# Causal attention feeding a mixture of experts on one core: the wide score products of most pairs as three float32r products with a split on GpSimd, separate loads, and a new order of steps

## The chip, the cores and the metric

The kernel runs on 1 core of one Trainium2 chip. The metric is the device time of a run in microseconds (us). In the profile PE is TensorE's matmul, PEld its weight load, DVE is VectorE, ACT ScalarE, POOL GpSimd, SP SyncE.

## The reference

Inputs are q, k and v of 4 batches x 12 heads x 448 positions x 64, and the weights of 8 experts. Attention first, causal and in float32:

```python
scores = scale * np.matmul(q, k.transpose(0, 1, 3, 2))
scores = np.where(mask, -1000000000.0, scores)
scores = scores - np.max(scores, axis=-1, keepdims=True)
attn = np.exp(scores)
attn = attn / (np.sum(attn, axis=-1, keepdims=True) + 1e-09)
return np.matmul(attn, v).astype(np.float32)
```

Its output, as 1792 tokens of 768 numbers, goes to a layer of experts: each token takes the one expert with the highest cosine similarity to an embedding, and the layer gives `gate * (relu(x @ w1[e]) @ w2[e])`, with w1 of 768 x 1024 and w2 of 1024 x 768.

## The kernel before

The 48 heads are worked as 24 pairs. A pair is one tile `raws[p % 4]` of 128 partitions x 2 x 448: q and k, transposed, the first head in partitions 0 to 63 and the second in 64 to 127. The 448 queries are cut into four chunks of 112; because of the causal mask, chunk i needs 112 x (i + 1) keys, so its scores are 112, 224, 336 or 448 columns wide. Each pair p passes through these steps, whose names carry the pair behind a point:

- LD loads q and k into `raws` and v into `vts`, both rings of four, by two transfers on SP's queue; SP waits in order, the transfer of v for the PV products of four pairs before.
- S0 to S3 are the scores of a chunk (S02 takes chunks 0 and 2 in one step), on PE in float32: for each head one product over 64 partitions, the two heads in the two halves of the array.
- M, on DVE, adds the mask, scales and takes the row maximum (in0 from PSUM, in1 the mask in SBUF); E, on ACT, is the exp with its sum. M21 is chunk 2, head 1.
- T transposes on PE; V (x and y halves) copies the transposes from PSUM to SBUF on ACT or DVE, as the order says (/A or /V).
- PV0 to PV3 are the products with v; VO copies the result. RC adds a constant to the sums on GpSimd (/G) or DVE (/V) and takes the reciprocal on DVE. X is a product that turns the result and adds router logits; XE and LE scale it by the reciprocals, on DVE.

After each batch of six pairs, WX writes x to DRAM on SP's queue, the R steps choose experts (Rc, on DVE, compares two operands in SBUF), and the q steps sum squares on GpSimd. After the third batch the commonest expert ("star") is known: LW and LL load its weights, W and Wl split w1 into a rounded float32r part and a float32r rest (W on ACT, Wl on GpSimd but for the last), A and B the same for w2 on ACT and DVE. The F and G steps are the first expert products; each float32 product there is already made of three float32r products. Behind them loops over up to 20 more tiles of tokens follow.

The order of all this on every engine is the string ORDER, written out by an offline search: a token is a step, its pair, a PSUM bank and an engine. An engine runs its own part of the list in that order and waits by semaphores. `h1` and `l1` are the tiles that later hold the split of w1. The 16 transposes of an identity ahead of ORDER only warm PE.

Of the kernel before, what the change touches and what calls it, by code (L numbers as in the profile page):

```python
# [45 lines left out]
V3x.1/A E20.2 S3.3:2 M00.3 M01.3 M20.3 M21.3 T0.2:1 E31.2 es6.0 V0x.2/A PV0.1:7 M31.3 es7.0 es8.0 VO.0/A E21.2 PV1.1
PV2.1 PV3.1 E30.2 RC.0/G M30.3 es9.0:2 esA.0 V0y.2/A E01.3 E00.3 T2.2:0 S02.4:2 V2x.2/A V2y.2/V X.0:1 M01.4 M00.4
E11.3 M20.4 M21.4 T3.2:0 E10.3 V3x.2/A V3y.2/A LD.5 XE0.0 XE1.0 LE1.0 E31.3 S3.4:2 LE0.0 E20.3 M30.4 S1.4:1 T0.3:0
PV0.2:6 E30.3 PV1.2 M31.4 V0x.3/V V0y.3/V RC.1/G M10.4 PV2.2 M11.4 E21.3 PV3.2 VO.1/V T2.3:0 LD.6 E01.4 E10.4 V2x.3/V
T3.3:1 V2y.3/A S1.5:2 V3x.3/V X.1:0 V3y.3/A E00.4 E30.4 M10.5 VO.2/A E31.4 S02.5:1 M11.5 S3.5:2 E11.4 LE0.1 PV0.3:7  # L50
M01.5 PV1.3 M00.5 E21.4 RC.2/G PV2.3 M21.5 XE0.1 M31.5 E21.5 XE1.1 M20.5 E20.4 LE1.1 PV3.3 E11.5 T0.4:0 M30.5 V0x.4/A
T2.4:1 T3.4:2 V0y.4/V V2y.4/A V2x.4/V X.2:0 V3y.4/V LD.7 S02.6:1 V3x.4/A E10.5 E00.5 RC.3/G XE1.2 RC.4/G S3.6:2 E20.5
LE0.2 M01.6 M20.6 LE1.2 E31.5 M00.6 E30.5 PV0.4:6 VO.3/A M30.6 XE0.2 PV1.4 PV2.4 PV3.4 M21.6 T2.5:1 M31.6 E01.5 T0.5:2
V2x.5/V E00.6 V0y.5/V S1.6:0 M11.6 V2y.5/A T3.5:1 M10.6 V0x.5/A V3x.5/V S3.7:2 S02.7:0 E20.6 V3y.5/A LD.8 M30.7 X.3:1
M31.7 LE1.3 E30.6 M20.7 E31.6 S1.7:2 LE0.3 E01.6 M00.7 PV0.5:7 E10.6 E21.6 VO.4/A XE1.3 M21.7 PV1.5 M01.7 PV2.5 E11.6
XE0.3 RC.5/G M11.7 PV3.5 T0.6:0 M10.7 V0y.6/V E21.7 T2.6:1 V2x.6/V E01.7 S1.8:2 V0x.6/A V2y.6/A M10.8 M11.8 X.4:0
LE1.4 T3.6:1 S02.8:2 E20.7 E31.7 VO.5/A XE0.4 XE1.4 LE0.4 M01.8 V3y.6/A M00.8 LD.9 X.5:0 M21.8 V3x.6/A M20.8 E21.8
XE1.5 T2.7:1 S3.8:2 RC.6/G E10.7 V2y.7/V E00.7 E11.7 E01.8 M30.8 PV0.6:7 PV1.6 V2x.7/V E30.7 PV2.6 XE0.5 PV3.6 LE1.5
LE0.5 T3.7:1 E20.8 M31.8 RC.7/G V3y.7/V LD.10 T0.7:0 VO.6/A S3.9:2 V0y.7/V V3x.7/A S1.9:1 R0.5:7 V0x.7/A M31.9 S02.9:0
M01.9 E31.8 M11.9 M30.9 M20.9 M10.9 E00.8 E30.8 PV0.7:6 E11.8 M21.9 PV1.7 E10.8 X.6:2 T2.8:1 M00.9 E30.9 T0.8:0  # L60
# [1096 lines left out]
```

## Time and profile before

| | |
|---|---|
| median of 3 runs | 479.69 us (478.72 to 480.52) |
| profiled execution | 477.16 us, span 475.4 us |
| granted TensorE clock, mean | 0.994 |
| PE busy | 458.1 us (96%) |
| DVE busy | 347.5 us (73%) |
| ACT busy | 296.0 us (62%) |
| GpSimd (POOL) busy | 111.6 us (23%) |

Times inside the profile are counted from the start of the span. A matmul's busy time includes its way through the array and overlaps with the next one's, so how fast products follow each other is read from starts, and a busy PE is not a PE at its peak. A wait is put down to what released the engine last.

### The profile page before, as it was taken

Reading aid. Unit: us, or ns where it says so; the run is one execution under the profiler, and the core shown is the slowest. Engines: PE = TensorE matmul, PEld = TensorE weight load, DVE = VectorE, ACT = ScalarE, POOL = GpSimd, SP = SyncE. Lnnn points to the kernel's source line nnn. Section 1 sums busy time; section 2 is a strip of 40 time slices with the busy share of each in tenths; the row PEclk is TensorE's granted clock in tenths of the full one; section 3 lists DMA queues with packets and bytes.
Section 4 is the critical chain, followed back from the end, with each engine's and each line's share of the span. In section 5 each row is a group of like instructions: output and inputs, shape, how many; then the busy total and the mean of one; then the engine's idle time right before and its main releaser. Section 6 shows DMA issues by size and latency. Waiting matters only on the chain. (4 is left out here: it accounts for less than half of the span.)

```text
span 475.4 us, 12096 instructions
## 1 busy us (share of the span) xinstructions
PE 458.1 (96%) x3868; PEld 375.7 (79%) x3868; DVE 347.5 (73%) x1023; ACT 296.0 (62%) x729; POOL 111.6 (23%) x121
## 2 busy tenths in 40 slices
PE   7999999998999989999999999999999999999993
PEld 5666666675776778888998899989989988988972
DVE  4989988897899799535778786919988456677441
ACT  6999998897999875311368662729476531171531
POOL 3000244056076633210031210202021020010121
PEclk9999999999999999999999999999999999999997
DMA  7333361363467753111779628287877411837881
GB/s 237 96 119 118 126 225 61 118 198 99 133 217 254 264 185 101 34 68 45 289 267 392 218 99 299 70 307 294 309 268 264 137 42 38 325 135 269 306 283 38
DMA packets 27376, 87.32 MB, mean 184 GB/s; under 512 B 2694, under 2 KB 3142, under 8 KB 27280
## 3 DMA queue, kind: packets, MB, share of 16 engines
q1 hardware_dynamic: 24160, 72.38, 43.8%
q0 software_dynamic: 3120, 13.77, 8.1%
q8 instruction: 47, 0.77, 0.7%
q14 instruction: 49, 0.40, 0.3%
HBM read 144.33 MB, written 12.58 MB: 330 GB/s over the span
## 5 line engine op out<-in xcount | busy, mean ns | idle before, releaser
L400 ACT ACTIVATE aq<-aq,mx 112x336 f32<-112x336 f32 (+3 forms) x192 | 99.9, 528 | 5.0 <-DVE mx L395 4.9
L395 DVE CUSTOM_DVE_ANT_0 aq<-bank,ar 112x336 f32<-112x336 f32 (+3 forms) x192 | 76.5, 442 | 14.5 <-PE bank L390 13.9
L851 POOL DMA_INDIRECT out_dram<-fa,isx x18 | 24.9, 1386 | 180.7 <-DVEq L1042 46.8
L390 PE MATMUL bank<-ak 64*112 64x112 f32 (+3 forms) x384 | 58.0, 414 | 2.3 <-DMA ak<-in_qk_dram 1.5
L433 PE MATMUL bank<-ap 112*64 112x112 f32 (+3 forms) x384 | 52.3, 408 | 0.0
L797 ACT COPY fa<-bank 128x512 f32<-128x512 f32 x28 | 15.2, 588 | 57.2 <-PE bank L738 40.2
L696 DVE STREAM_TRANSPOSE turned<-fa 32x256 f32<-32x256 f32 x112 | 48.8, 435 | 1.5
L433 PEld LDWEIGHTS bank<-ap 112*64 112x64 f32 x384 | 24.5, 136 | 25.0 <-issue 15.5
L1005 DVE TENSOR_TENSOR wl<-fa,wh 128x1024 fp32r<-128x1024 f32 x36 | 41.5, 1220 | 3.1 <-PE bank L739 1.6
L422 ACT COPY ap<-bank 112x384 f32<-112x384 f32 (+2 forms) x87 | 38.6, 481 | 7.0 <-PE bank L418 5.5
L418 PEld LDWEIGHTS bank<-idt,aq 64*112 64x112 f32 (+1 forms) x960 | 33.5, 131 | 11.8 <-issue 2.7
L418 PE MATMUL bank<-idt,aq 48*112 48x48 f32 (+1 forms) x960 | 38.5, 219 | 0.9 <-DVE mx L395 0.7
L601 POOL DMA_INDIRECT fa<-xd,ig x21 | 23.2, 1103 | 64.5 <-PE bank L669 52.5
L400 ACT ACTIVATION_READ_ACCUMULATOR aq<-aq,mx 112x1 f32 x192 | 37.8, 197 | 0.0
L390 PEld LDWEIGHTS bank<-ak 64*112 64x112 f32 x384 | 28.3, 175 | 12.0 <-DVE mx L395 4.8
L1004 ACT CAST wh<-fa 128x1024 fp32r<-128x1024 f32 x36 | 34.9, 1047 | 3.5 <-PE bank L740 1.6
L740 PE MATMUL bank<-wh,akr 128*128 128x512 f32 x84 | 33.0, 393 | 0.8 <-DVE akr L650 0.8
L422 DVE COPY ap<-bank 112x384 f32<-112x384 f32 (+2 forms) x57 | 28.7, 521 | 6.6 <-PE bank L418 6.2
L738 PE MATMUL bank<-wh,akr 128*128 128x512 f32 x84 | 33.0, 393 | 0.0
L740 PE MATMUL bank<-wh,apr 128*128 128x512 f32 x84 | 32.9, 391 | 0.0
L739 PE MATMUL bank<-wl,akr 128*128 128x512 f32 x84 | 32.8, 391 | 0.0
L739 PE MATMUL bank<-wl,aor 128*128 128x512 f32 x84 | 32.8, 390 | 0.0
(312 smaller groups left out, 1076.0 us busy)
## 6 DMA issues: line engine op xcount, KB each, us to landing
fa<-in_w_dram SPq DMA_DIRECT2D x76, 768.0 KB
fa<-in_w_dram SPq DMA_DIRECT2D x54, 1024.0 KB
ak<-in_qk_dram SPq DMA_DIRECT2D x24, 448.0 KB
ap<-in_vv_dram SPq DMA_DIRECT2D x24, 224.0 KB
xd<-fa SPq DMA_DIRECT2D x3, 1344.0 KB
fa<-in_w_dram SPq DMA_DIRECT2D x6, 512.0 KB
xd<-fa SPq DMA_DIRECT2D x1, 1120.0 KB
fa<-xd,ig POOLq DMA_INDIRECT x21, 6.6
```

Source lines behind the costliest of these rows:

```text
L390: pe.matmul(o, raws[p % 4][rows, 0, CP * i : CP * i + CP], raws[p % 4][rows, 1, :n], start=True, stop=True, tile_position=(D * h, 0), skip ...
L395: v.tensor_tensor_reduce(out=Ps[p % 2][i, h], in0=st.pop(("sp", p, i, h)), in1=mask[i], scale=-0.125, scalar=3e38, op0=ALU.add, op1=ALU.mi ...
L400: ac.activation(x, x, AF.Exp, bias=mxs[p % 3][:, h, i : i + 1], scale=-1.0, accum_out=sums[p % 3][:, h, i : i + 1])
L418: pe.transpose(t[:, h, k], Ps[p % 2][i, h][r, c * CP : c * CP + CP], idt[r, r], tile_position=(r.start, 0))
L422: copy()(PTs[p % 2][:, :, slice(*GROUPS[n]), ROWS[half]], st["pt", p, n][half])
L433: pe.matmul(st["o", p][64 * h : 64 * h + 64, CP * c : S], vts[p % 4][:, c, 64 * h : 64 * h + 64], PTs[p % 2][:, h, RUNS[c]], start=c == 0, ...
L696: v.transpose(xk[32 * j : 32 * j + 32, :, q : q + 32], blocks[q : q + 32, :, j])
L738: pe.matmul(acc[j], xh[:, k], wh[k][:, o], start=k == ends[0], stop=False)
L739: pe.matmul(acc[j], xh[:, k], wl[k][:, o], start=False, stop=False)
L740: pe.matmul(acc[j], xl[:, k], wh[k][:, o], start=False, stop=k == ends[1])
L1004: ac.copy(h[k], r[:, k])
L1005: v.tensor_tensor(l[k], r[:, k], h[k], op=ALU.subtract)
```

## The change

It does four things. For pairs 1 to 20, the scores of chunks 2 and 3 (336 and 448 columns wide) are no longer one float32 product per head, but three float32r products summed in PSUM: high x high, high x low, low x high. The high and low parts are made by two new GpSimd steps, `hi` (a copy that rounds to float32r) and `lo` (the difference), over 672 columns: the queries from 224 on and all keys. They live in the first three tiles of `h1` and `l1`, used in turn. The load of q and k (LDr) is a step apart from that of v (LDv), and pair 0's is cut in two, with the first 224 columns (LDa) in front. And ORDER is new throughout; some of its lines are shown.

```diff
 ORDER = """
-EE.0 LD.0 S1.0:0 es0.0 M11.0 E11.0 LD.1 M10.0 E10.0 S02.0:1 M00.0 M01.0 M20.0 E00.0 M21.0 S3.0:2 M31.0 E01.0 S1.1:0
...
-M11.16 M10.16 T2.14:0 VO.13/V V2x.14/A X.12:1 S02.16:2 XE1.12 WX.11 V2y.14/A LE0.12 LE1.12 XE0.12 R1.11 M21.16 LD.17
...
+LDa.0 LDr.0 S1.0:1 EE.0 es0.0 S3.0:0 S02.0:2 M11.0 M10.0 M31.0 LDr.1 M30.0 M20.0 M21.0 S1.1:1 M01.0 hi.1 E10.0 E31.0
...
+V3y.1/V es4.0 M10.3 hi.3 V3x.1/A lo.3 S3.3:2 M11.3 es5.0 E31.2 S02.3:0 es6.0 M30.3 E01.2 hi.4 E20.2 T3.2:1 es7.0 M01.3
...
+LDv.15 E20.15 q0.11 E11.15 LDr.17 PV3.13 T0.14:1 V0y.14/V R0.11:6 LDr.19 T3.14:0 VO.13/A V0x.14/A V3y.14/A V3x.14/A
+X.12:2 XE0.12 S02.16:1 hi.17 E10.15 LE1.12 XE1.12 E01.15 E30.15 LE0.12 M20.16 M01.16 X.13:0 M21.16 hi.18 WX.11 E31.15
...
+M10.16 R2.11 RC.14/G lo.17 XE1.13 RC.15/G S1.17:2 XE0.13 qa0.11 V0y.15/A E20.16 M10.17 M11.17 T3.15:1 S3.17:0 V3y.15/A
...
-        @step("LD")
-        def _(p):
-            sy.dma_start(raws[p % 4], qk[p])
-            sy.dma_start(vts[p % 4], vv[p])
+        HALF = slice(0, 2 * CP), slice(2 * CP, S)
+        step("LDa", FIRST)(lambda p: sy.dma_start(raws[0][:, :, HALF[0]], qk[0][:, :, HALF[0]]))
+
+        @step("LDr")
+        def _(p):
+            c = slice(0, S) if p else HALF[1]
+            sy.dma_start(raws[p % 4][:, :, c], qk[p][:, :, c])
+
+        step("LDv")(lambda p: sy.dma_start(vts[p % 4], vv[p]))
+
+
+        SPLIT = range(1, NP - 3)
+        his, los = ([x[:, : 2 * CP + S] for x in xs_[:3]] for xs_ in (h1, l1))
+
+        def late(p):
+            return raws[p % 4].rearrange("p a s -> p (a s)")[:, 2 * CP :]
+
+        step("hi", SPLIT)(lambda p: g.tensor_copy(his[p % 3], late(p)))
+        step("lo", SPLIT)(lambda p: g.tensor_tensor(los[p % 3], late(p), his[p % 3], op=ALU.subtract))
 
         def scores(p, chunks):
...
                 n = CP * (i + 1)
-                for h in range(2):
-                    rows = slice(D * h, D * h + D)
-                    st["sp", p, i, h] = o = sp[h][:CP, at : at + n]
-                    pe.matmul(o, raws[p % 4][rows, 0, CP * i : CP * i + CP], raws[p % 4][rows, 1, :n],
-                              start=True, stop=True, tile_position=(D * h, 0), skip_group_check=len(chunks) > 1)
+                x, y = his[p % 3], los[p % 3]
+                terms = ((x, x), (x, y), (y, x))
+                for k, (a, b) in enumerate(terms if p in SPLIT and i > 1 else ((None, None),)):
+                    for h in range(2):
+                        rows = slice(D * h, D * h + D)
+                        st["sp", p, i, h] = o = sp[h][:CP, at : at + n]
+                        if a is None:
+                            q, keys = raws[p % 4][rows, 0, CP * i : CP * i + CP], raws[p % 4][rows, 1, :n]
+                        else:
+                            q, keys = a[rows, CP * (i - 2) : CP * (i - 1)], b[rows, 2 * CP : 2 * CP + n]
+                        pe.matmul(o, q, keys, start=k == 0, stop=a is None or k == 2, tile_position=(D * h, 0),
+                                  skip_group_check=True)
                 at += n
```

## Rows read from the trace of the kernel before

**Rows 1.** Busy time in two stretches: us, then busy us (instructions) of each engine, PE's clock, DMA.

```profile
6.00:155.00 149.00, 145.16 (x1982) 97.24 (x1980) 131.78 (x613) 139.28 (x477) 47.26 (x54) 1.00 0.48 154
...
190.00:320.00 130.00, 129.55 (x707) 116.16 (x707) 83.95 (x147) 57.82 (x91) 22.08 (x19) 1.00 0.52 188
```

**Rows 2.** The masks' line: count, ns min/median/max, first and last start.

```profile
L395 DVE CUSTOM_DVE_ANT_0 aq<-bank,ar x192: 257/424/626, 6.3 to 154.6; 112x224 f32<-112x224 f32 x48, 112x112 f32<-112x112 f32 x48, 112x336 f32<-112x336 f32 x48, 112x448 f32<-112x448 f32 x48
```

**Rows 3.** Order of time around 104 us: start us, us, engine, line, operation.

```profile
102.75 0.73 PE L390 MATMUL bank<-ak 64*112 64x336 f32 x4
...
103.31 0.92 PE L457 MATMUL bank<-ar,ao 64*112 64x72 f32 x16
...
104.06 0.61 PE L418 MATMUL bank<-idt,aq 64*112 64x64 f32 x16
...
104.60 2.11 PE L433 MATMUL bank<-ap 112*64 112x448 f32 x16
```

**Rows 4.** Waits of ACT, 6 to 155 us: us in total, times, longest.

```profile
ACT ap L422 <- PE bank L418: 5.5, 7, 1.7
ACT aq L400 <- DVE mx L395: 4.9, 4, 3.2
```

**Rows 5.** Waits of DVE, 6 to 155 us.

```profile
DVE aq L395 <- PE bank L390: 13.9, 19, 5.3
```

**Rows 6.** Order of time, float32r expert products of 512 columns.

```profile
167.21 0.39 PE L739 MATMUL bank<-wl,akr 128*128 128x512 f32 x1
...
167.44 0.39 PE L740 MATMUL bank<-wh,akr 128*128 128x512 f32 x1
```

**Rows 7.** GpSimd's operations by form, 6 to 155 us: busy us, mean ns.

```profile
L537 POOL TENSOR_TENSOR fa<-fa 112x768 f32<-112x768 f32 x9 | 16.4, 1822 | 0.6
...
L537 POOL TENSOR_TENSOR fa<-fa 112x192 f32<-112x192 f32 x3 | 1.8, 595 | 0.2
```

**Rows 8.** Operations by form, whole span.

```profile
L395 DVE CUSTOM_DVE_ANT_0 aq<-bank,ar 112x336 f32<-112x336 f32 x48 | 23.0, 499 | 2.8 <-PE bank L390 2.8
...
L286 POOL COPY ar<-idt 64x384 f32<-64x384 f32 x2 | 1.0, 498 | 0.1
```

**Rows 9.** The split of w1, on two engines: ns min/median/max.

```profile
L579 POOL TENSOR_TENSOR wl<-fa,wh x5: 2356/2382/2411, 152.0 to 168.8; 128x1024 fp32r<-128x1024 f32 x5
...
L579 DVE TENSOR_TENSOR wl<-fa,wh x1: 1174/1174/1174, 164.3 to 164.3; 128x1024 fp32r<-128x1024 f32 x1
```

**Rows 10.** Order of time around 169 us.

```profile
168.84 2.40 POOL L579 TENSOR_TENSOR wl<-fa,wh 128x1024 fp32r<-128x1024 f32 x1 [0.25 <-ACT wh L578]
...
169.53 2.53 DVE L873 TENSOR_TENSOR aqr<-fa,akr 128x768 fp32r<-128x768 f32 x1 [0.16 <-ACT akr L872]
```

**Rows 11.** The line of that DVE operation, later: ns min/median/max.

```profile
L873 DVE TENSOR_TENSOR apr<-fa,apr x4: 937/939/941, 180.7 to 183.9; 128x768 fp32r<-128x768 f32 x4
```

**Rows 12.** Order of time around 98 us.

```profile
98.10 2.89 POOL L540 TENSOR_TENSOR fa<-fa 112x768 f32<-112x768 f32 x2 [3.83 <-DVE fa L462]
...
98.37 0.50 DVE L395 CUSTOM_DVE_ANT_0 aq<-bank,ar 112x336 f32<-112x336 f32 x1
```

**Rows 13.** Order of time on SP's queue, 85 to 112 us.

```profile
99.22 0.38 SPq L475 DMA_DIRECT2D xd<-fa  x1
99.65 0.48 SPq L378 DMA_DIRECT2D ak<-in_qk_dram  x1
```

**Rows 14.** Order of time, 108.4 to 110.4 us.

```profile
108.46 1.39 PE L390 MATMUL bank<-ak 64*112 64x448 f32 x8 [1.28 <-DMA ak<-in_qk_dram]
...
110.24 0.48 ACT L422 COPY ap<-bank 112x384 f32<-112x384 f32 x1 [1.74 <-PE bank L418]
```

**Rows 15.** Order of time at the start.

```profile
4.06 1.06 PE L975 MATMUL bank<-idt 128*128 128x128 f32 x4
...
5.30 1.95 PE L390 MATMUL bank<-ak 64*112 64x224 f32 x14 [0.18 <-DMA ak<-in_qk_dram]
```

**Rows 16.** Waits of GpSimd, 6 to 155 us.

```profile
POOL sum L444 <- ACT aq L400: 68.7, 14, 8.3
```

More of the change, by code (lines that the diff above doesn't have):

```diff
@@ L46 @@
[L46 to L60, printed above, removed]
@@ L111 @@
-A5.23 B4.23 H1.23:4 GA.23 HLb.23 B5.23 G4.23 Q0.23 xta.23:3 xha.23 xtb.23:5 G5.23 B6.23 B7.23 xhb.23 H2.23 xla.23
-G6.23 xlb.23 IS.23 B0.23
+LDa.0 LDr.0 S1.0:1 EE.0 es0.0 S3.0:0 S02.0:2 M11.0 M10.0 M31.0 LDr.1 M30.0 M20.0 M21.0 S1.1:1 M01.0 hi.1 E10.0 E31.0
+lo.1 E30.0 T3.0:0 E20.0 LDr.2 M00.0 hi.2 E11.0 M10.1 S02.1:2 M11.1 V3y.0/A V3x.0/V S3.1:1 LDv.0 E00.0 E01.0 E21.0
+M01.1 M00.1 T0.0:0 lo.2 M21.1 E21.1 V0y.0/A M20.1 T2.0:2 M30.1 LDr.3 E20.1 V0x.0/A LDr.5 M31.1 V2y.0/V V2x.0/A S02.2:1
+T2.1:0 S3.2:2 PV0.0:7 es1.0 E01.1 M31.2 V2y.1/A E31.1 E10.1 M20.2 PV1.0 V2x.1/A E11.1 S1.2:0 M30.2 E00.1 M10.2 PV2.0
@@ new lines @@
+M11.2 E30.1 hi.5 PV3.0 T0.1:2 M00.2 E30.2 M01.2 T3.1:0 M21.2 S1.3:1 LDv.1 LDr.4 LDr.6 V0y.1/A V0x.1/A es2.0 es3.0
+V3y.1/V es4.0 M10.3 hi.3 V3x.1/A lo.3 S3.3:2 M11.3 es5.0 E31.2 S02.3:0 es6.0 M30.3 E01.2 hi.4 E20.2 T3.2:1 es7.0 M01.3
+M20.3 es8.0 M31.3 lo.4 E11.2 PV0.1:6 PV1.1 V3x.2/A PV2.1 M21.3 PV3.1 RC.0/G E21.2 LDv.2 E00.2 es9.0:2 M00.3 E10.2
+esA.0 T2.2:2 RC.1/G V3y.2/A VO.0/A T0.2:0 V2y.2/A V0y.2/A V2x.2/V S02.4:1 V0x.2/V LDr.7 X.0:2 M00.4 E01.3 M21.4 S3.4:0
+PV0.2:7 E11.3 M01.4 E10.3 E20.3 E31.3 LE0.0 PV1.2 LDv.3 E30.3 LE1.0 XE1.0 M20.4 E00.3 E21.3 XE0.0 PV2.2 M30.4 M31.4
@@ new lines @@
+VO.1/V T3.3:1 RC.2/G lo.5 LDv.4 S1.4:0 V3y.3/V M11.4 M10.4 T0.3:2 PV3.2 V0y.3/V V3x.3/A S1.5:1 E20.4 V0x.3/A LDr.8
+T2.3:0 S3.5:2 VO.2/A E21.4 V2y.3/A M10.5 E10.4 M11.5 E11.4 V2x.3/V M30.5 S02.5:1 M31.5 hi.6 lo.6 PV0.3:6 M21.5 M00.5
+M01.5 X.1:2 E30.4 E00.4 M20.5 XE1.1 E11.5 E30.5 E01.4 T2.4:0 X.2:1 V2y.4/V LDv.5 E00.5 RC.3/G PV1.3 V2x.4/V XE1.2
+LE1.2 E31.4 LE0.1 LDr.9 PV2.3 E01.5 LE0.2 XE0.1 E10.5 PV3.3 LE1.1 T0.4:0 XE0.2 V0x.4/A V0y.4/V T3.4:2 V3y.4/V V3x.4/A
+S1.6:1 hi.8 M10.6 M11.6 S3.6:0 M31.6 S02.6:2 hi.7 E20.5 E21.5 M30.6 T0.5:1 PV0.4:7 M01.6 E31.5 M20.6 V0x.5/A M21.6
@@ new lines @@
+lo.7 T2.5:0 M00.6 V0y.5/A V2y.5/V T3.5:1 S02.7:2 RC.5/G VO.3/A V2x.5/A RC.4/G LDr.10 lo.8 V3x.5/A V3y.5/A S3.7:0 E01.6
+M00.7 E30.6 M01.7 M21.7 E20.6 M20.7 M30.7 X.3:1 M31.7 LE1.3 XE1.3 S1.7:2 M11.7 XE0.3 PV1.4 PV2.4 PV3.4 E10.6 E11.6
+LDv.6 E00.6 E21.6 M10.7 LE0.3 PV0.5:6 hi.9 T0.6:1 E31.6 V0y.6/A V0x.6/A LDr.11 VO.4/V T2.6:0 V2x.6/A X.4:2 V2y.6/V
+E00.7 T3.6:1 E11.7 S02.8:0 PV1.5 E10.7 V3x.6/A E01.7 LDv.7 V3y.6/A PV2.5 lo.9 XE0.4 LE1.4 M00.8 M01.8 RC.6/G PV3.5
+M20.8 XE1.4 LE0.4 E31.7 LDv.8 E00.8 S1.8:2 S3.8:1 M21.8 VO.5/V M11.8 X.5:0 M10.8 T0.7:2 XE1.5 PV0.6:7 E21.7 E21.8
@@ new lines @@
+LE0.5 hi.11 M31.8 E10.8 E20.7 PV1.6 E30.7 V0y.7/A LE1.5 V0x.7/V PV2.6 XE0.5 hi.10 E20.8 M30.8 PV3.6 T3.7:0 LDr.12
+T2.7:2 VO.6/V V3x.7/A V3y.7/V V2y.7/A V2x.7/V S3.9:1 S02.9:0 M31.9 M30.9 E30.8 M01.9 E01.8 lo.10 S1.9:2 E31.8 q0.5
+M11.9 E11.8 E01.9 PV0.7:7 hi.12 T3.8:1 M10.9 M21.9 X.6:2 R0.5:6 PV1.7 PV2.7 V3x.8/A V3y.8/A E30.9 PV3.7 XE0.6 RC.7/G
+T0.8:1 M00.9 q3.5 q2.5 LE1.6 XE1.6 WX.5 q1.5 E31.9 LE0.6 M20.9 VO.7/A V0x.8/V LDr.13 T2.8:2 V0y.8/A V2x.8/A E11.9
+E20.9 S3.10:0 V2y.8/V S02.10:1 E21.9 M30.10 M00.10 M01.10 LDv.10 E00.10 RC.8/G S1.10:2 PV0.8:7 M11.10 M31.10 M21.10
@@ new lines @@
+PV1.8 PV2.8 LDv.9 PV3.8 E00.9 lo.12 R1.5 E10.9 M20.10 T0.9:0 M10.10 R2.5 lo.11 R3.5 E21.10 S1.11:1 R4.5 X.7:2 M11.11
+V0x.9/A LDr.14 qa1.5 M10.11 R5.5 V0y.9/A XE0.7 E30.10 T2.9:0 XE1.7 T3.9:1 V2x.9/A LE1.7 RK.5 LE0.7 V2y.9/A V3y.9/A
+V3x.9/V VO.8/A E20.10 S02.11:2 S3.11:0 E31.10 RC.9/V X.8:1 M21.11 M30.11 E01.10 E11.10 M31.11 Rg.5/V hi.14 M01.11
+qa0.5 PV0.9:7 M00.11 M20.11 E10.10 qb.5 PV1.9 PV2.9 E21.11 LE0.8 XE0.8 XE1.8 E01.11 T2.10:2 LE1.8 R6.5 E30.11 T0.10:0
+V2y.10/V V0y.10/V T3.10:1 V2x.10/A S3.12:2 V3y.10/V V0x.10/A LDr.15 LDv.11 E00.11 M30.12 V3x.10/A S02.12:0 S1.12:1
@@ new lines @@
+R8.5 PV3.9 M20.12 E31.11 E11.11 PV0.10:6 M10.12 M11.12 M01.12 hi.13 E20.11 M00.12 qc.5 PV1.10 VO.9/A E10.11 M31.12
+M21.12 T2.11:1 V2x.11/V T0.11:2 E11.12 V2y.11/A V0x.11/A LDr.16 lo.13 T3.11:0 V0y.11/V V3y.11/V V3x.11/A S02.13:1
+S3.13:2 RC.10/G M00.13 X.9:0 hi.15 R7.5 RC.11/G M20.13 PV0.11:7 lo.14 PV2.10 M21.13 M30.13 XE0.9 XE1.9 Ra.5 LDv.12
+E00.12 E31.12 E30.12 LE1.9 E20.12 E30.13 qd.5 E21.12 PV3.10 LE0.9 E10.12 M01.13 PV1.11 E01.12 M31.13 T3.12:1 V3y.12/A
+Rc.5 T2.12:2 qe.5 S1.13:0 LDv.14 V2y.12/A PV2.11 V2x.12/A V3x.12/V M10.13 PV3.11 T0.12:1 VO.10/V S02.14:2 LDv.13
@@ new lines @@
+M00.17 M21.17 V2x.15/A VO.14/A E01.16 E11.17 M20.17 M30.16 X.14:2 T2.16:1 PV0.15:7 M31.16 PV1.15 V2x.16/V LE0.14
+E00.16 LE1.14 E10.16 XE0.14 PV2.15 XE1.14 E30.16 hi.20 E31.16 T3.16:0 V2y.16/V E11.16 E10.17 hi.19 T0.16:1 V3y.16/V
+E01.17 E20.17 S1.18:2 V3x.16/V E00.17 V0y.16/V LDv.17 M10.18 qb.11 V0x.16/A RK.11 LDr.21 S3.18:0 M11.18 R6.11 E30.17
+S02.18:1 M01.18 lo.19 E31.17 T0.17:2 M00.18 LDv.16 qc.11 E21.17 M30.18 V0x.17/A LDr.22 PV3.15 M31.18 PV0.16:6 PV1.16
+E10.18 M20.18 V0y.17/A RC.16/G M21.18 T2.17:2 S1.19:1 T3.17:0 VO.15/A E01.18 V2y.17/A E21.18 R8.11 E11.18 V2x.17/V
@@ new lines @@
+V3y.17/A M11.19 E20.18 M10.19 S3.19:2 X.15:1 E30.18 RC.17/G lo.20 V3x.17/V S02.19:0 R7.11 qd.11 PV2.16 qe.11 PV3.16
+M31.19 M01.19 M00.19 PV0.17:7 PV1.17 Ra.11 Rb.11 PV2.17 E11.19 Rc.11 E10.19 M30.19 PV3.17 M20.19 E31.18 T3.18:2 M21.19
+VO.16/A XE0.15 LE0.15 E00.18 E30.19 VO.17/A LE1.15 X.16:0 XE1.15 T0.18:1 V3y.18/V LE1.16 LE0.16 LDv.18 V3x.18/A XE0.16
+X.17:2 XE1.16 XE1.17 LE0.17 T2.18:0 E21.19 V0x.18/A V0y.18/A LE1.17 LDr.23 XE0.17 LDv.19 E00.19 S02.20:1 S3.20:2 q3.17
+q1.17 E01.19 M00.20 M01.20 V2y.18/A M21.20 V2x.18/A R9.11/G LDv.20 E00.20 M20.20 M30.20 T0.19:0 E01.20 M31.20 E21.20
@@ L113 @@
+B7.23 xla.23 B0.23 xhb.23 H2.23 G6.23 xlb.23 IS.23
 """
```

80 lines of the change are left out of this document (27 added, 53 removed).

## Prediction

> **What bounds the kernel now.** I read the windows of busy time first, to find the stage that the change touches, then the waits of each engine in that stage, then the order of time.
>
> From 6 to 155 us the 24 pairs of heads pass through attention. Nothing there has much to spare: ACT is busy 139.28 of 149 us, DVE 131.78, PE 145.16, GpSimd only 47.26 [rows 1]. PE's figure includes the tails of overlapped matmuls, so I count its work from start times instead. The masks run from 6.3 to 154.6 us [rows 2], one pair every 148.3/24 = 6.2 us. PE's work on a pair comes from one unbroken stretch [rows 3]: 336 columns of scores for both heads take 103.31 - 102.75 = 0.56 us, so the 1120 columns of a pair take 1.87; the X products 0.75; 16 transposes 0.54, so 40 take 1.35; the PV products 2.11 with their tail. That is 6.1 of 6.2 us. PE and ACT are both nearly full.
>
> Who waits for whom says which leads. ACT's idle time is 9.7 us; 5.5 of it is spent on transposes from PE, and 4.9 on masks, mostly at the start [rows 4]. DVE waits 13.9 us for scores, 5.3 of it before the first one [rows 5]. So PE's lateness is what ACT and DVE still lose to.
>
> Behind attention PE is busy 129.55 of 130 us [rows 1]: that stage has a fixed length here, it starts when attention lets it, and what attention gains should reach the end.
>
> **The change, part by part.**
>
> *Wide scores.* For pairs 1 to 20 the chunks of 336 and 448 columns become three float32r products. Now 784 columns cost 784/336 x 0.56 = 1.31 us per pair. A float32r product of 512 columns starts 0.23 us after the one before it [rows 6], 0.45 ns a column. Three passes over 784 columns cost 1.06 us, if two heads in two halves of the array overlap as the float32 passes do. Then PE saves 0.25 us a pair, 20 x 0.25 = 5.0 us. No row shows a float32r product on half of the rows. If the heads do not overlap, the price is 2.12 us, 0.81 more per pair, +16.2 us. Those are the bounds, and I take the overlap, because the float32 products of the same shape show it.
>
> *The split on GpSimd.* `lo` takes two inputs of 672 columns. Such an operation costs 0.595 us at 192 columns and 1.822 at 768 [rows 7], so 672 come to 1.62. `hi` is a copy: 0.498 us for 384 columns [rows 8], by proportion 0.87. A copy that rounds is not in the trace; below I put 0.5, the copy of 384, above 1.62, the price of `lo`. 2.5 us x 20 = 50 us, and GpSimd goes from 47 to 97 of 149 us. It does not become the bound by its sum, so the split is costed at nothing; its cover is GpSimd's idle time, and without that a pair would pay up to 2.5 us.
>
> On DVE the same work would be cheaper: 1.17 us against 2.38 for 1024 columns [rows 9]. The Trainium skill, GPSIMD Engine Reference, section "Engine selection", says elementwise work belongs on VectorE, GpSimd being about twice as slow with two inputs, which speaks against this placement. The trace agrees with the ratio (2.38 to 1.17). By the rule `lo` would move to DVE and add some 0.8 us per pair there, which DVE, busy 88%, has not; so I leave the sum as it is.
>
> *What GpSimd does to DVE beside it.* An operation of DVE with both inputs in SBUF normally takes 0.94 us [rows 11], and took 2.53 while GpSimd subtracted [rows 10]: it stood still until GpSimd ended. The masks, with one input in PSUM, do not suffer: 0.50 us beside GpSimd's work [rows 12], 0.499 in the mean [rows 8]. The Trainium skill, SBUF — State Buffer, section "Who interferes with whom", has just this split: two SBUF inputs contend with GpSimd's reads, one does not; the trace agrees (2.53 against 0.50). Only Rc, two times inside the stretch, is of that kind. Up to 1.6 us each, against 0 if they miss: I take 0.5 us in all.
>
> *Loads.* One queue on SP now holds q/k, v and x. A q/k load issued at 99.65 followed the write of a batch of x (448 x 768 float32, 1.4 MB) issued at 99.22 [rows 13]; PE then stood 1.28 us until 108.46 for a q/k load, and ACT 1.74 until 110.24 for the transposes that came late after it [rows 14]. By the list it is that of pair 17, S3.17 being next. In the new list LDr.17, LDr.18 and LDr.19 are all ahead of WX.11, and LDv, which must wait for PV of four pairs before, no longer stands ahead of the next q/k. I take 1.7 us; at least 0, if the next wait takes its place.
>
> *Start.* The first score begins at 5.30, released by its load; the last four warm-up transposes begin at 4.06 and last 1.06 us with their tails [rows 15]. At 0.21 us each (1.06/5, the tail counted as one) PE could go on at 4.9. LDa.0 carries half of the load and stands ahead of EE, so I take these 0.4 us; at least 0, if the load is no earlier.
>
> *The order.* ACT gets 108 of the copies out of PSUM where it had 106, DVE 60 where it had 62, and three sums move from GpSimd to DVE. Under 1 us each way on an engine; I take nothing.
>
> *What new waits it brings.* GpSimd works its queue in order. It now waits 68.7 us, 14 times, for exps before the sums of RC [rows 16]; `hi` and `lo` will stand behind such waits, and RC behind `hi`, `lo` and the squares. Behind RC's sum the reciprocal waits at the head of DVE's queue, and with it the masks. In the list lo.17 follows RC.14 and S3.17 comes soon after; hi.3 and lo.3 are right in front of S3.3.
>
> *Sum.* PE is not alone at its limit, so its 5.0 us are not all kept. If ACT lost nothing, the stage would shorten by 9.7; if ACT's other work held it, by none of the 5.0. I keep 3.0, a little over half, since ACT loses 5.5 us to PE, of which 1.7 is in the load term. 3.0 + 1.7 + 0.4 - 0.5 = 4.6 us. The profiled execution took 477.16 us with a span of 475.4; it becomes 472.6. It ran 2.5 us under the median of the runs, 479.69, so on that scale I forecast 479.7 - 4.6 = **475.1 us**.
>
> **The rivals.** About 0.5%, 2.4 us, is what a measurement of this kernel can tell from no change.
>
> - *It is hidden.* ACT is busy 93.5% of the stage, as full as PE; a faster score then only waits for a free buffer. Left are load and start, 2.1 less 0.5: 478.1 us, or 479.7 with a new load wait. For it: ACT's total is unchanged. Against it: 5.5 us of waits for PE.
> - *The halves do not overlap* (slower). PE's pair grows from 6.1 to 6.9 us, past the pace of 6.2: 20 x 0.7 to 20 x 0.81 = +14 to +16, less 2: about 492 us. It decides from a pair of products over 1.25 times the overlapped price (1.31/1.06). Against it: the float32 rows.
> - *GpSimd is late* (slower). A late `lo`, or a late RC, costs its successor up to 1.6 us. Three such waits eat the gain; seven, a third of the pairs, give 7 x 1.6 - 4.6 = +6.6: 486 us. For it: the queue in order, two thirds full. Against it: most loads and `hi` stand a pair or more ahead of use.
>
> **How the numbers follow.** Forecast 0.55 (its own range 469.5 to 477.3: from all of ACT's idle time and the start gone, 10.2, to the 2.4 that can be told), hidden 0.24, GpSimd late 0.13, halves apart 0.08. The first is faster, the second the same, the last two slower: 0.55, 0.24, 0.21. For 8 in 10 I reach from 470 to 482.5: it takes in the hidden case and the mild half of GpSimd's lateness, and leaves out the other half, the halves apart, and the last of the low end, about 0.17.
>
> **What would show it.** In the new profile, float32r score passes of 448 columns should follow each other for both heads every 0.2 us; `lo` should cost 1.6 us and `hi` 0.9; GpSimd some 95 us before 155; the wait for a q/k load near 108 us should be gone; ACT's wait for transposes should fall from 5.5 us to 3 or less; the last mask should end near 150 us and the first expert product start that much earlier. I am wrong if PE's score waits name GpSimd for several us, if DVE's reciprocals wait for its sums, if score passes of the two heads take turns, or if the gain at the last mask is lost before the expert products begin.

## The result, and the profile after

The changed kernel takes **473.59 us** (median of 4 runs, 472.34 to 474.32) against 480.1 for the kernel before beside it (4 runs): ratio **0.9867 [0.9834, 0.9899]**, 6.4 us less. The forecast was 475.1 with a gain of 4.6. A second series gave 0.9878 [0.9859, 0.9898].

Windows of the profile after; first the stage of [rows 1], then its thirds:

```profile
6.00:155.00 149.00, 145.83 (x2130) 105.31 (x2128) 136.20 (x624) 143.37 (x493) 96.52 (x94) 1.00 0.50 162
6.00:60.00 54.00, 51.99 (x740) 37.10 (x738) 49.72 (x228) 51.16 (x181) 28.40 (x32) 1.00 0.48 155
60.00:110.00 50.00, 49.40 (x767) 37.34 (x765) 45.19 (x214) 47.88 (x167) 40.05 (x36) 1.00 0.49 156
110.00:155.00 45.00, 44.44 (x633) 30.88 (x635) 41.29 (x186) 44.32 (x148) 28.07 (x28) 1.00 0.53 178
```

The 149 us now hold some us of the stage behind attention, since attention is shorter. GpSimd's 47 us are 96.5, as predicted, but not evenly: in the middle third it is busy 40.05 of 50 us. The masks' line and the split's lines, of the same profile (the answer of [rows 2], and GpSimd's operations by form as in [rows 7]):

```profile
L420 DVE CUSTOM_DVE_ANT_0 aq<-bank,ar x192: 210/424/625, 6.3 to 150.3; 112x224 f32<-112x224 f32 x48, 112x448 f32<-112x448 f32 x48, 112x336 f32<-112x336 f32 x48, 112x112 f32<-112x112 f32 x48
```

```profile
L397 POOL TENSOR_TENSOR wl<-ak,wh 128x672 fp32r<-128x672 f32 x20 | 32.4, 1626 | 1.1
...
L396 POOL CAST wh<-ak 128x672 fp32r<-128x672 f32 x20 | 14.7, 746 | 18.7 <-PE bank L415 11.4 <-DMA ak<-in_qk_dram 6.8 <-POOL wh L396 0.4
```

The last mask starts at 150.3 instead of 154.6 [rows 2], the first at 6.3 as before. Waits of ACT, DVE and GpSimd, 6 to 155 us, to be read against [rows 4, 5, 16]:

```profile
ACT fa L348 <- DMA fa<-in_emb_dram: 3.0, 1, 3.0
ACT aq L425 <- DVE mx L420: 2.3, 5, 0.8
ACT ap L447 <- PE bank L443: 1.6, 5, 0.4
...
DVE aq L420 <- PE bank L415: 10.6, 14, 5.3
...
POOL sum L469 <- ACT aq L425: 13.0, 7, 3.3
```

ACT's wait for transposes fell from 5.5 to 1.6 us, DVE's for scores from 13.9 to 10.6, and GpSimd's for exps from 68.7 to 13.0: it now has other work to do before it reaches the sums. No wait of PE for a q/k load is left. Order of time on PE, the scores of chunk 3 of one pair, with the row that ends them:

```profile
63.13 0.44 PE L415 MATMUL bank<-wh 64*112 64x448 f32 x2
63.41 0.37 PE L415 MATMUL bank<-wl,wh 64*112 64x448 f32 x2
63.62 0.37 PE L415 MATMUL bank<-wh,wl 64*112 64x448 f32 x2
63.83 0.35 PE L415 MATMUL bank<-ak 64*112 64x112 f32 x4
```

Each of the first three rows is one pass for both heads (x2); their records start 4 ns apart. The heads overlap, and a pass of 448 columns takes 0.28, 0.21 and 0.21 us from start to start.

### The profile page after: what moved, and what is told of

Same layout as the page of the kernel before. It is cut to its first block, busy times and chain, and to the rows that moved or that the text cites. A ratio compares the mean times of both kernels' runs of the same rounds, so it can differ in the third digit from the quotient of the medians.

```text
span 472.0 us, 12320 instructions
## 1 busy us (share of the span) xinstructions
PE 454.4 (96%) x3948; PEld 380.9 (81%) x3948; DVE 349.3 (74%) x1024; ACT 295.9 (63%) x731; POOL 158.0 (33%) x158
## 5 line engine op out<-in xcount | busy, mean ns | idle before, releaser
L425 ACT ACTIVATE aq<-aq,mx 112x224 f32<-112x224 f32 (+3 forms) x192 | 99.9, 529 | 2.4 <-DVE mx L420 2.3
L876 POOL DMA_INDIRECT out_dram<-fa,isx x18 | 25.0, 1387 | 181.1 <-DVEq L1067 60.4
L420 DVE CUSTOM_DVE_ANT_0 aq<-bank,ar 112x224 f32<-112x224 f32 (+3 forms) x192 | 76.0, 441 | 12.1 <-PE bank L415 10.6
L458 PE MATMUL bank<-ap 112*64 112x448 f32 (+3 forms) x384 | 53.2, 409 | 0.0
L626 POOL DMA_INDIRECT fa<-xd,ig x21 | 23.7, 1129 | 62.8 <-PE bank L694 51.2
L443 PEld LDWEIGHTS bank<-idt,aq 64*112 64x112 f32 (+1 forms) x960 | 33.2, 131 | 13.9 <-ACT aq L425 4.4
L458 PEld LDWEIGHTS bank<-ap 112*64 112x64 f32 x384 | 23.8, 136 | 20.7 <-issue 12.6
L397 POOL TENSOR_TENSOR wl<-ak,wh 128x672 fp32r<-128x672 f32 x20 | 32.4, 1626 | 1.1
L763 PE MATMUL bank<-wh,aor 128*128 128x512 f32 x84 | 32.7, 389 | 0.0
L415 PE MATMUL bank<-ak 64*112 64x224 f32 (+3 forms) x224 | 31.3, 359 | 0.5 <-DVE ar L492 0.3
```

Of the source, the lines that this page charges most:

```text
L397: step("lo", SPLIT)(lambda p: g.tensor_tensor(los[p % 3], late(p), his[p % 3], op=ALU.subtract))
L420: v.tensor_tensor_reduce(out=Ps[p % 2][i, h], in0=st.pop(("sp", p, i, h)), in1=mask[i], scale=-0.125, scalar=3e38, op0=ALU.add, op1=ALU.mi ...
L425: ac.activation(x, x, AF.Exp, bias=mxs[p % 3][:, h, i : i + 1], scale=-1.0, accum_out=sums[p % 3][:, h, i : i + 1])
L443: pe.transpose(t[:, h, k], Ps[p % 2][i, h][r, c * CP : c * CP + CP], idt[r, r], tile_position=(r.start, 0))
L458: pe.matmul(st["o", p][64 * h : 64 * h + 64, CP * c : S], vts[p % 4][:, c, 64 * h : 64 * h + 64], PTs[p % 2][:, h, RUNS[c]], start=c == 0, ...
L763: pe.matmul(acc[j], xh[:, k], wh[k][:, o], start=k == ends[0], stop=False)
```

## The experiments

Besides the time, three marks of the profiled execution are compared: the attention stretch (start of the first mask to end of the last), the start of IG (the step that hands the rows over to the expert stage; one row of DVE), and the span. They are single executions; two of the same kernel differ by 0.3 us in the attention stretch, 1.1 at IG and 2.3 in the span. Two kernels leave out what the output needs, so that past IG their expert stage may work on other rows: products_unsplit, whose later pairs multiply stale parts, and tail_as_before. In some of the profiles the granted clock of TensorE falls from 1.00 to 0.50, the lower of its two levels (1.2 instead of 2.4 GHz), for part of the attention stretch or of the way from it to IG: in old_order_split, lo_twice, lo_on_dve, old_order_apart, load17_first and tail_as_before. In the others, the two of before and the two of the changed kernel among them, it stays at 1.00 up to IG.

| kernel | us, median (runs) | ratio to before | attention | IG | span |
|---|---|---|---|---|---|
| before | 479.69 (3) | | 148.6 | 178.6 | 475.4 |
| before_again | 479.44 (12) | 0.9994 [0.9969, 1.002] | 148.9 | 179.7 | 477.7 |
| load17_first | 477.93 (12) | 0.9977 [0.9958, 0.9996] | 147.4 | 179.2 | 476.0 |
| old_order_apart | 481.92 (8) | 1.0056 [1.0032, 1.008] | 152.3 | 184.3 | 481.4 |
| old_order_apart_2 | 477.87 (12) | 0.9981 [0.9954, 1.0008] | 147.7 | 178.1 | 474.6 |
| old_order_split | 489.48 (6) | 1.0218 [1.0168, 1.0267] | 160.2 | 189.3 | 485.5 |
| new_order_f32 | 474.31 (6) | 0.988 [0.9849, 0.991] | 146.7 | 175.2 | 473.0 |
| split_unused | 476.25 (7) | 0.9918 [0.9889, 0.9947] | 147.3 | 176.1 | 473.1 |
| products_unsplit | 472.32 (5) | 0.9856 [0.9837, 0.9876] | 143.8 | 172.4 | 470.2 |
| after | 473.59 (4) | 0.9867 [0.9834, 0.9899] | 144.3 | 173.2 | 472.0 |
| after_again | 473.4 (5) | 0.9878 [0.9859, 0.9898] | 144.6 | 173.8 | 472.8 |
| lo_twice | 486.05 (4) | 1.013 [1.0074, 1.0186] | 156.7 | 185.3 | 483.8 |
| lo_on_dve | 486.47 (4) | 1.0158 [1.0102, 1.0214] | 158.0 | 186.9 | 484.3 |
| tail_as_before | 488.4 (6) | 1.0196 [1.0156, 1.0236] | 144.4 | 178.8 | 485.6 |

**The two kernels again**, nothing edited: the scale.

> The kernel before, unchanged, as a yardstick. Ratio 1.000 within 0.4%. The profiled execution of before took 477.16 us where the timed runs took 478.7 to 480.5; if that was one lucky execution, a new profile has a span near 478 and its extra 2 to 3 us lie behind attention (first expert product at 166 us again); if the profiled time is the rule for profiled executions, the span is 475.4 again.

> The changed kernel once more, beside the kernels it is to be compared with. Both theories: 0.9867 of the kernel before, some 473.5 us; masks from 6.3 to about 150.6 us. If the part of the gain that is read off the timed runs and not off the masks (6.4 against 4.3 us) was the luck of one execution, the span of this profile lies 1 to 1.5 us above 472.0 with the masks ending at the same time.

Both repeat. The second execution of the changed kernel has the attention stretch within 0.3 us and a span 0.8 longer.

**New list and loads apart, scores as before** (no split).

```diff
-SPLIT = range(1, NP - 3)
+SPLIT = range(0)          # and all hi, lo taken out of the list
```

> The new order and the separate loads, but all scores as one float32 product, and no split on GpSimd. My theory (PE's relief is worth about 3 of the gain): 3 us slower than the changed kernel, 476.5, ratio to before 0.993. Rival (the relief is hidden behind ACT; order and loads do it all): as fast as the changed kernel, 473.6, ratio 0.987. If the order hangs on the short scores: slower than before, over 480.

Measured: 0.988, over 5 us of gain without a single float32r score. By the time that is the rival's forecast (0.987) and not mine (0.993); what the products do has to be read from the attention stretch, below. ACT's wait for transposes in it, 6 to 155 us, is already down:

```profile
ACT ap L445 <- PE bank L441: 2.1, 8, 0.4
```

So the fall from 5.5 us, which I named as the mark of faster scores, is mostly the list's and the loads' doing.

**The split without the products**, and **the products without the split**: the two other corners.

```diff
 # split_unused: split runs, scores float32
-for k, (a, b) in enumerate(terms if p in SPLIT and i > 1 else ((None, None),)):
+for k, (a, b) in enumerate(((None, None),)):
 # products_unsplit: split for pairs 1 to 3 alone
-step("hi", SPLIT)   step("lo", SPLIT)
+step("hi", range(1, 4))   step("lo", range(1, 4))
```

> The changed kernel with hi and lo still run on GpSimd but not used: all scores are one float32 product each. Against the run without the split it prices the split's side effects (GpSimd's port and queue) alone. My theory: 0.5 us, so 477 against 476.5; if GpSimd's work holds up DVE or the sums of RC, 2 us or more over the run without it.

> The changed kernel with GpSimd's split done for pairs 1 to 3 alone; the pairs after them multiply the stale parts that lie in the buffers, so their scores aren't theirs (the time is what is looked at). This is the fourth corner beside the changed kernel (split and products), the kernel with the split but float32 products, and the one with neither. Theory A (products save 3.0 us in attention, the split costs 0.6 to 2.0 by side effects): 471.5 to 473 us, 0.6 to 2.0 us under the changed kernel, and 2.5 to 3 under the kernel with neither. Rival B (the products save nothing that ACT doesn't hold back, and what moved was order alone): equal to the kernel with neither, 474.3. Rival C (the split costs nothing because GpSimd is idle there, as the prediction had it for all but 0.5 us): equal to the changed kernel, 473.5.

In the attention stretch the products take off 2.9 us without the split (146.7 to 143.8) and 2.7 to 3.0 with it (147.3 to 144.6 and 144.3); the split adds 0.5 to 0.8, with the products or without. Each effect comes out the same in the other's presence. By the timed ratios the products are worth 1.2 us without the split (0.988 to 0.9856) and 1.9 to 2.4 with it; the intervals reach 1 to 1.5 us to each side, so they don't contradict the profiles. In the attention stretch it is as theory A of products_unsplit has it; in time that kernel is 2.0 us under the one with neither, and not 2.5 to 3. split_unused is 1.9 us slower than new_order_f32 by the medians, near the 2 us that its text gave to the other side.

Where in the stretch the split's 0.6 us arise can be read from the starts of the masks. Counted from the first mask, those of split_unused are up to 1.1 us behind those of new_order_f32 in the first 20 us, and from the 33rd to the last, the 192nd, 0.61 to 0.67 us: over all the pairs in between the split costs nothing. Within those 20 us one small operation of DVE with both inputs in SBUF, a step of `es`, stands beside `lo` in the changed kernel, from about 19 us:

```profile
19.34 1.63 POOL L397 TENSOR_TENSOR wl<-ak,wh 128x672 fp32r<-128x672 f32 x1
...
19.52 1.47 DVE L323 TENSOR_TENSOR es<-es 8x1 f32<-8x1 f32 x1
```

It takes 1.46 us in the second profile of that kernel too, and 0.14 to 0.15 us in new_order_f32. What the engines do in the attention stretch, windows of new_order_f32, products_unsplit and after:

```profile
5.87:152.57 146.70, 144.29 (x1976) 96.29 (x1972) 132.14 (x612) 139.62 (x477) 46.21 (x50) 1.00 0.48 155
```

```profile
5.71:149.47 143.76, 140.62 (x2056) 101.93 (x2052) 132.31 (x612) 139.41 (x479) 53.30 (x56) 1.00 0.48 159
```

```profile
6.31:150.60 144.29, 141.30 (x2056) 101.88 (x2052) 132.87 (x612) 138.73 (x477) 92.66 (x90) 1.00 0.48 157
```

PE's time falls by 3.67 us with the products, ACT's by 0.21; the stretch follows PE by 2.94. ACT's idle time, 7.08 us with float32 scores, becomes 4.35.

**The split in the old list**: the old order, each load cut in two but left in its place, hi and lo put right behind the load (or behind the last wide score that reads their buffers).

```diff
-... LD.4 ...
+... LDr.4 LDv.4 hi.4 lo.4 ...
```

> The old order with the split and the three float32r products put in: q/k and v loads stay together at their old places, hi and lo of a pair follow its load. My theory: PE's relief shows in any order, 477 us, ratio 0.994, less what late lo steps cost. Rival (hidden): 480, ratio 1.00. Rival (GpSimd late): the scores of some pairs wait for lo, 482 or more, and PE's score waits name GpSimd.

It is 10 us slower than before: the same products and the same split. Its waits of DVE and of PE, 6 to 165 us, name GpSimd:

```profile
DVE R L470 <- POOL sum L469: 4.6, 4, 3.1
...
PE bank L415 <- POOL wl L397: 2.4, 2, 1.2
PE bank L415 <- POOL wh L396: 2.0, 2, 1.9
```

PE's weight loads wait another 5.5 us for the two parts. That is the rival "GpSimd is late", in its place and its waits, and the new list is what keeps the change out of it. But the waits are not the whole price. PE's clock in two stretches of this run, and the order of time on PE at the start of the second and in it:

```profile
11.30:18.10 6.80, 6.42 (x72) 6.11 (x70) 5.48 (x22) 4.45 (x15) 6.30 (x6) 0.50 0.47 119
113.70:127.30 13.60, 10.55 (x84) 7.25 (x82) 5.67 (x26) 5.82 (x19) 13.11 (x11) 0.50 0.11 37
```

```profile
113.45 0.49 PE L415 MATMUL bank<-wh 64*112 64x448 f32 x2 [1.88 <-POOL wh L396]
115.14 0.71 PE L415 MATMUL bank<-wl,wh 64*112 64x448 f32 x2 [1.19 <-POOL wl L397]
...
118.70 0.57 PE L415 MATMUL bank<-wl,wh 64*112 64x448 f32 x2
119.08 0.57 PE L415 MATMUL bank<-wh,wl 64*112 64x448 f32 x2
```

Just before each of the two falls PE had stood for a part of the split (1.25 us until 10.93, 1.88 until 113.45). A pass of 448 columns then takes 0.38 us from start to start and not 0.21. An estimate from these rows: the 20.4 us at 0.50 cost at most 20.4 x (1 - 0.21/0.38) = 9 of the 11.6 us by which the attention stretch is longer than in before. The timed runs have it too: their mean granted clock is 0.966 to 0.981, against 0.989 to 0.998 in those of before. So late parts cost the wait, and then a slower PE. My places for hi and lo were not searched for; other places in the old list might cost less.

**Where the load term comes from.** First the list before with one step moved.

```diff
-... XE1.12 WX.11 V2y.14/A ... M21.16 LD.17
+... XE1.12 LD.17 WX.11 V2y.14/A ... M21.16
```

> The kernel before, with the load of pair 17 moved ahead of the write of batch WX.11 in the list, and nothing else. Theory A (the prediction's load term: PE's 1.28 us and ACT's 1.74 us at 108 to 110 us are what the stage loses): 1.7 us less, 477.9 us, ratio 0.9965; the wait for a q/k load near 108 us gone from PE's waits. Rival B (the next wait takes its place): no difference within 0.5 us, the wait gone all the same.

0.9977: 1.1 us, of the 1.7 in my sum. The q/k wait of PE is gone and the attention stretch is 1.2 to 1.5 us shorter. But IG starts no earlier than in the two profiles of before. Behind attention ACT waits longer for a load of an expert's weights, 150 to 182 us, in load17_first and, for comparison, in before:

```profile
ACT wh L578 <- DMA fa<-in_w_dram: 3.7, 2, 3.3
```

```profile
ACT wh L578 <- DMA fa<-in_w_dram: 2.9, 2, 1.6
```

That takes a part of the gain back: the last of these casts starts 0.5 us earlier than in before, and not 1.2. The rest goes with the clock, which in this profile fell behind attention:

```profile
171.80:175.20 3.40, 3.12 (x7) 2.48 (x8) 3.13 (x19) 2.26 (x6) 0.00 (x0) 0.50 0.18 67
```

PE had stood 1.05 us until 170.18, and stood again, 0.78 us until 172.07, when it fell. A product of 512 columns takes 0.43 us there instead of 0.23. The one at 172.07 starts 0.5 and 1.6 us earlier than the same one in the two profiles of before; from it to IG it is 7.2 us, and 6.1 in both of before.

Then all loads apart in the old list, q/k early, scores float32; the second version holds the early loads back until that of pair 3 is out.

```diff
-... LD.1 ... S3.0:2 ... LD.2 ... LD.3 ... LD.4
+... LDr.1 LDv.1 ... S3.0:2 LDr.4 ... LDr.5 ... LDr.2 LDv.2 ... LDr.3 LDv.3 ... LDr.6 ... LDv.4     # _apart
+... LDr.1 LDv.1 ... S3.0:2 ... LDr.2 LDv.2 ... LDr.3 LDv.3 LDr.4 LDr.5 ... LDr.6 ... LDv.4         # _apart_2
```

> The kernel before with its list as it is, except that each q/k load stands right behind the last score of four pairs earlier, and v's load stays where the pair's load stood. All scores float32, no split. It differs from the kernel that has the new list, loads apart, and float32 scores in the list alone. Theory A (the loads are what made that one faster by 5.2 us; the list itself is worth nothing, as the prediction costed it): 474.5 us. Rival B (the list is worth the larger part): 478 us, the load term of 1.7 and no more. Rival C (q/k loads that start early collide with the writes of x and with v): no faster than before, 479.5.

> As the kernel with the old list and loads apart, but the early q/k loads begin behind the load of pair 3, so that those of pairs 4 and 5 no longer stand in the queue ahead of that of pair 2 (that cost 3.5 us at 17 us). Scores float32, no split. Theory A (loads apart are worth what the one load ahead of the write is worth, and the rest of the gain is the list): 478 us, as with that one load moved. Rival B (loads apart are worth the larger part of the 5.2 us that the new list with loads apart and float32 scores gains): 475 to 476 us, the masks shorter than 146.9 us from first to last.

The first was my mistake: two early loads stood in the queue ahead of that of pair 2, and PE waited, 6 to 155 us (the clock then was at 0.50 from 17.4 to 20.7 us):

```profile
PE bank L413 <- DMA ak<-in_qk_dram: 3.9, 2, 3.5
```

Without that, loads apart are worth 0.9 us (0.9981), no more than the one load moved. The masks say the same: counted from the first mask, those of load17_first and of old_order_apart_2 keep to those of before (a constant 0.3 and 0.5 us behind from 10 us on), are 1.5 us earlier from one step on, the mask that starts at 109.5 us in before, and stay so to the end. Theory A: the rest of what new_order_f32 gains, 0.9981 to 0.988 or 4.8 us by the ratios (some 2 either way), is the list's order, with the cut load of pair 0, which that kernel has too. By the marks it is 1.0 in the attention stretch and 2.9 at IG. Part of the 4.8 goes with the clock: the three timed runs of old_order_apart_2 with a mean granted clock of 0.996 or more took 476.1 to 476.8 us, the six of new_order_f32, all at 0.996, 474.1 to 474.9, some 2 us less.

**How much cover GpSimd has.**

```diff
 # lo_twice
-g.tensor_tensor(los[p % 3], late(p), his[p % 3], op=ALU.subtract)
+for _ in range(2): g.tensor_tensor(los[p % 3], late(p), his[p % 3], op=ALU.subtract)
 # lo_on_dve
-g.tensor_tensor(los[p % 3], ...)
+v.tensor_tensor(los[p % 3], ...)
```

> The changed kernel, with each subtraction of the split done twice on GpSimd: 20 times 1.63 us more, so that GpSimd is busy some 129 of the 149 us of attention instead of 96.5. Theory A (the split's cost is a matter of when a part is ready and of sums that come late, and it grows before GpSimd is full): 1 to 5 us more than the changed kernel, with DVE's reciprocals waiting for GpSimd's sums. Rival B (there is cover enough, as the prediction had it): 473.5, no change. Rival C (GpSimd late, at the prediction's price of 1.6 us each time): 486 us or more.

> The changed kernel, with the subtraction of the split on DVE instead of GpSimd, in the same place of the list: 20 times some 0.8 us more on DVE (busy 136 of 149 us in attention), 20 times 1.63 us less on GpSimd. Theory A (DVE is as near to its limit as ACT, so it pays nearly in full): 8 to 16 us more than the changed kernel, 482 to 489 us. Rival B (DVE has slack enough, and what GpSimd no longer holds up is given back): within 2 us of 473.5 us; that is what the rule that elementwise work belongs on VectorE would make of it.

Twice costs 12.6 us (486.05 against 473.4): 32.5 us of work, of which GpSimd hides some 60%. The middle third, and the waits of DVE and PE, of lo_twice:

```profile
60.00:110.00 50.00, 46.01 (x708) 34.26 (x703) 43.73 (x188) 44.70 (x152) 46.92 (x40) 1.00 0.47 153
```

```profile
DVE R L474 <- POOL sum L473: 5.7, 6, 2.0
PEld bank L419 <- POOL wl L400: 5.6, 5, 2.0
...
PE bank L419 <- POOL wl L400: 4.2, 3, 1.7
```

GpSimd is busy 46.92 of 50 us there. The cost is not spread over the pairs. Counted from the first mask, the masks fall 3.7 us behind those of the changed kernel by 30 us, less than 0.1 more up to 72 us, 4.5 from there to 92, and 4.3 between 109 and 133. In the first and the last of these stretches the clock fell too:

```profile
12.30:19.10 6.80, 6.79 (x60) 5.13 (x58) 4.87 (x26) 4.51 (x15) 3.72 (x4) 0.50 0.51 171
128.40:131.80 3.40, 3.40 (x34) 3.17 (x36) 1.92 (x8) 2.66 (x10) 3.32 (x3) 0.50 0.01 3
```

Just before, PE had stood 1.73 us for a `lo` and 1.80 for a mask. By the estimate made for old_order_split, these 10.2 us cost at most 4.6 of the 12.4 us by which the attention stretch is longer. Of the theories, rival C's time and theory A's mechanism: A's 1 to 5 us were too few, and neither counted a fall of the clock.

On DVE the subtraction takes half as long, and costs 13.1 us:

```profile
L397 DVE TENSOR_TENSOR wl<-ak,wh 128x672 fp32r<-128x672 f32 x20 | 18.6, 931 | 0.0
```

18.6 us more on DVE lengthen the attention stretch by 13.7. Theory A. (The clock fell once, from 41.1 to 44.5 us, behind a stand of PE of 1.02 us for a mask; reckoned as above, at most 1.5 of the 13.7.) The Trainium skill, GPSIMD Engine Reference, section "Engine selection", has GpSimd about twice as slow with two inputs: the trace agrees (1626 to 931 ns, 852 in the median). What the rule would make of it here, elementwise work on VectorE, loses by 13 us, because DVE has not that much idle time to give.

**The end of the list.** The 168 steps behind the last mask, put in the order that they have in the old list.

```diff
-... T3.22:0 YI.17 T2.22:2 E21.23 ... LW3.17 ... LW5.17 ... LW4.17 ...
+... LDv.23 W1.17 YI.17 E30.23 Wl1.17 ... LW5.17 ... LW4.17 ... LW3.17 ...
```

> The changed kernel, with the 168 steps that follow its last mask put in the order that they have among themselves in the list before; everything up to the last mask is as in the changed kernel. The time from the last mask to the input of the expert stage being known (the step IG) is 22.7 to 23.1 us in five kernels with the new list and 23.9 to 25.7 in four with the old one. Theory A (the new list is worth 1 to 2.6 us behind attention, which the prediction costed at nothing): masks end at 150.6 as they do now, IG comes 1 to 2.6 us later, and the kernel takes 474.5 to 476 us. Rival B (the difference there is made by what precedes it: which loads and buffers are still in use when attention ends): no change from 473.5.

Attention ends as it did (last mask ends at 150.3), and IG starts at 178.8, 5.0 to 5.6 us later than in the changed kernel: more than either theory. PE stood 1.77 us until 153.9 and 1.61 until 164.3, and behind each the clock was at 0.50, from 155.5 to 158.9 and from 165.8 to 169.1; at 0.43 us for a product of 512 columns instead of 0.23, an estimate is that this cost at most 3.1 of the 5.0 to 5.6. So the order there can cost that much, but this end is not the old list's: it stands behind another beginning. In this order the kernel doesn't compute the reference's output, and its expert stage works on other rows, so its time past IG says nothing.

## Why the prediction was right, point by point

The forecast (faster, 475.1) held, but that its sum of 4.6 us came near the measured 6.4 is in part luck. By the times the largest part is one that the sum left out, the order, and the split and the products together add only 0.1 to 0.6 us to new_order_f32 (0.988 to 0.9878 and 0.9867), which is inside the intervals. In the attention stretch they take off 2.1 to 2.4 us, for a forecast 2.5 (3.0 - 0.5): there the account is right. From IG to the end new_order_f32 takes 297.8 us and the two profiles of the changed kernel 298.8 and 299.0; the two of before differ by 1.2 there, so where the rest of that gain went stays open.

- *Wide scores, kept gain 3.0.* Right: 2.7 to 3.0 in the attention stretch. Both factors were off. From start to start over all records, 448 columns take 0.81 us as float32 and 0.69 as three passes, 336 columns 0.57 and 0.53 (the first pass of a chunk is longer). That saves 0.16 us a pair, 3.2 in all, and not 5.0; and nearly all of it is kept in that stretch, not 0.6 of it. The halves do overlap, as the float32 rows had it.
- *"It is hidden".* Wrong for the attention stretch, which followed PE although ACT's work stayed nearly the same. ACT's 93.5% left it 9.4 us of idle time in the stretch, and PE's lateness was in it.
- *Load term, 1.7.* 1.5 at the wait itself, in three kernels; by the times 1.1 [0.2, 2.0] with that load alone, 0.9 with all loads apart. The mechanism was right. "What attention gains should reach the end" did not hold in the profile of load17_first: a weight load and a fall of the clock behind attention took the gain back before IG. In that of old_order_apart_2, where the clock stayed at 1.00, IG is 0.5 and 1.7 us earlier than in those of before.
- *Start, 0.4.* Open. The first score begins at 5.05 instead of 5.30 [rows 15], the first mask at 6.31 instead of 6.29. The load of emb now follows, and ACT waits 3.0 us for it. Over all profiles the first mask starts at 5.7 to 6.3 us in the eight with the new list's beginning and at 6.2 to 6.8 in the six with the old: 0.4 less in the mean, which is also what the two executions of before differ by.
- *The order, costed at nothing.* This is the step that failed. I counted operations per engine and found under 1 us of difference. Order changes who waits for whom, not the counts: 4.8 us by the ratios, 2.9 at IG, some 2 between runs at the same granted clock. One part is in attention, one between the last mask and IG. From the end of the last mask to IG the seven kernels that keep the new list's end take 22.6 to 22.9 us, whatever attention took (143.8 to 158.0). The old list takes 23.7 to 24.1 in the two profiles of before and in old_order_apart_2, so the new one is worth about 1.2 us there. It takes 25.3 and 25.5 in old_order_apart and load17_first, the two in which the clock fell on that way (to 0.50 from 177.8 to 181.1 and from 171.8 to 175.2), and 22.9 in old_order_split, which stays open. Which waits the new order removed, step by step, no run takes apart.
- *The split, nothing but 0.5 of side effect.* Prices right (`lo` 1.63 for 1.62, `hi` 0.75 for 0.87); side effect 0.5 to 0.8 in the attention stretch, 0.5 to 1.8 by the ratios. It doesn't come from Rc, as I had it: Rc, three times in the stretch and not two, takes 683 to 693 ns in the changed kernel and 684 to 691 without the split. Nor is Rc the only operation there with two inputs in SBUF: the step of `es` has them too, and stood still beside `lo`. So the mechanism was right and the operation wrong; that this one makes up the whole cost is not shown.
- *"GpSimd is late", 0.13.* It did not happen, but only just: it is what the split does in the old list (489.5) and with one more subtraction per pair (486.1). "97 of 149" was a mean; the middle third was at 80%. The rival's price, up to 1.6 us for each wait, left out the fall of the clock behind such waits.

The marks that I named: the passes, the split's prices, GpSimd's 95 us, the q/k wait, the last mask near 150 and the first expert product (161.6 us, 4.6 earlier) came as said. ACT's wait for transposes fell as said, but new_order_f32 shows that it fell for another reason. One slip in the sums: 9.7 and 0.4 us, at the low end of the forecast's own range, are 10.1 and not 10.2, which changes nothing.

## What to carry to other kernels

A new order of the same work is a change with a price of its own: run the new order alone before crediting what came with it, and run the new work in the old order to see whether it needs the new one. An idle engine's cover is read from its busiest stretch and from who waits behind it in its queue, not from its mean over a stage. Where two engines are both near full, ask which one's idle time names the other; the gain from the one that is waited for came through almost whole in its stage. And look at the granted clock before a loss is put down to waits alone: in several variants here the loss was part waiting and part a slower PE after it.

## What the runs showed of the hardware

Three float32r products on 64 rows of the array run for two heads at once, a pass of 448 columns every 0.21 us behind a first of 0.28; against one float32 product of the same columns (0.81 us for the chunk) three of them save only 15%. GpSimd's rounding copy of 672 columns took 0.746 us, less per column (1.11 ns) than the plain copy of 384 (0.498, 1.30 ns a column [rows 8]), so proportion overstated it. The subtraction on DVE took 852 ns in the median and up to 1517. An operation of 8x1 on DVE with both inputs in SBUF took 1.47 us beside GpSimd's subtraction and 0.15 without it. In the six profiles with a fall of the granted clock up to IG, PE had stood for 0.6 to 3.5 us shortly before it; not every such stand ended in a fall (the 1.28 us until 108.46 in before did not). At 0.50 a float32r pass of 448 columns on 64 rows took 0.38 us instead of 0.21, one of 512 on 128 rows 0.43 instead of 0.23.
